# Sliding-window attention feeding a gated FFN: bursts of the fourth unit, weight groups by halves, and the first tile's output groups, on one core

## Chip, core and metric

The kernel runs on one core of a Trainium2 chip. The core has a matrix engine (TensorE, in the profile PE, with its weight loads apart as PEld), a vector engine (VectorE, DVE), an activation engine (ScalarE, ACT), a general engine (GpSimd, POOL) and a queue engine (SyncE, SP) that issues transfers; POOL and ACT issue transfers as well. Each engine works through its own instructions in the order in which the program gives them, and waits on semaphores for the others. The metric is the time of one execution in microseconds of device time. The median of three runs before the change is 301.93 us (301.90 to 302.15).

## What is computed

Causal attention with a window of 64 positions, over 8 batches of 8 heads, 576 positions and head dimension 64; its output, heads side by side, is the input of a feed-forward layer with a ReLU gate (4608 tokens, model width 512, inner width 1536).

```python
scores = (1 / sqrt(64)) * q @ k.T                # per batch and head, 576 x 576
mask = (rel >= 0) & (rel < 64)                   # rel = query position - key position
attn = exp(scores - max) / (sum + 1e-9)          # masked scores are -1e9
x = (attn @ v) as [4608, 512]
out = (maximum(x @ w_gate, 0) * (x @ w_val)) @ w_out
```

Inputs and output are float32. The kernel converts to float16 in the transfers and accumulates in float32.

## The kernel before, in words

**Tiles and units.** The tokens are cut into tiles: four of 384 tokens (tiles 0 to 3), then six of 512. Attention for the first tiles goes by *units* of 192 tokens, three windows of 64 for all 8 heads; units 0 to 2 are batch 0, units 3 to 5 batch 1, units 6 to 8 batch 2. Units 0 and 1 feed tile 0, units 2 and 3 tile 1, and so on. The third unit in the text is unit 2, the fourth unit 3, the fifth to eighth are units 4 to 7. Later attention goes by *quads* of four windows.

**A unit's steps.** `qk_load` (L179, POOL's queue) brings q and k into one of four places of the tile `nats`; `qk_trans` (L199, DVE) transposes them into qT and kT, four transposes a batch: k twice, q twice, a half of the heads each. `u_st` (L265, PE) makes the scores in four banks, `u_exp` (L299, ACT) takes the exponential, `u_mask` (L306, DVE) multiplies by the window's mask, and `u_pv` (L336, PE) multiplies by v into two banks. `u_recip` (L350), `u_norm` (L357) and `u_turn` (L379), all on DVE, normalise and transpose the result into the tile's `xt`. `v_load` (L205, POOL's queue) brings v, and `v_spread` copies some of its rows to the other half of the partitions, on an engine (L215) or by a transfer on SP (L217). `behind_masks` (L312) puts tiny copies on POOL that wait for a unit's masks.

**The FFN of tiles 0 and 1** is the plain product. `hidden` makes gate and value columns in groups: w columns of 128 that fit a bank together (one for 384 tokens, two for 192), four matmuls a column over the 512 of the input (L589). For each block of four columns all gate groups come first (`relu`, L572, ACT), then all value groups (`gate`, L575, DVE). Tile 1 is done in two halves of 192 tokens, because its two units end apart. `output` (L1023) multiplies by w_out: twelve matmuls of 512 columns for 128 tokens, in cuts; then ACT copies the bank (L1035) and SP stores it (L1036). From tile 2 on `fast_hidden` (L634) uses seven products of halves in place of eight. Its operands are sums that `w_form` (L528), `o_form` (L788) and `x_form` (L506) make on DVE and POOL. In the last six tiles the output (`SevenOut`, L847) does the same; there the names P1 to P7 are products, v0 and v1 the attention values of the next tile (`values`, L465), s0 and s1 scores, h1 the start of the next tile.

**Weights.** `w_load` (L159) brings w_gate and w_val in blocks of four columns. Each block is two transfers: a=0 brings the input's chunks 0 and 1, a=1 chunks 2 and 3. `w_done` holds one due time for each column, and `w_need` lets the plan wait for it.

**What sets the order.** A small planner, the `Weaver` W, writes the order out. It has a clock that the code advances by what PE's matmuls are meant to take, and a heap of due actions. `W.at(T, fn)` puts an action in; when the matmul code calls `W.advance`, due actions are issued before the next matmul. So a planned time places an instruction among PE's matmuls, and among the instructions of its own engine; on the chip only queues and semaphores decide. `one_bank` hands out banks 0 to 3 in turn, `two_banks` banks 4 and 5 or 6 and 7; both first issue what still has to read the bank. In the trace the banks 0 to 7 are not told apart.

Of the kernel before, what the change touches and what calls it, by code (L numbers as in the profile page):

```python
# [47 lines left out]
def kernel(  # L48
# [10 lines left out]
    nc = tc.nc  # L59
# [94 lines left out]
    def w_load(wt, src, f0, f1, landed):  # L154

        if wt is not wo:
            ns = slice(128 * f0, 128 * f1)
            for a in range(2):
                nc.gpsimd.dma_start(wt[:, 2 * a:2 * a + 2, ns], src.rearrange("(a p e) n -> a p e n", a=2, e=2)[a, :, :, ns])  # L159
        if wt is wo:  # L160
            nc.gpsimd.dma_start(wo[:, f0:f1], src.rearrange("(c p) n -> p c n", p=128)[:, f0:f1])
        w_done.update(((wt.name, f), landed) for f in range(f0, f1))

    def w_need(wt, f):
        while (wt.name, f) not in w_done:
            W.pop()
        W.advance(w_done[wt.name, f])

# [238 lines left out]
    def part_written(banks):  # L407
        written.update((id(to), 0) for to in banks)
# [145 lines left out]
        while normed[0] < n:  # L554
            W.pop()

    def hidden(t, spans, f0=0, f1=NF, each=1):

        if t not in gs:
            gs[t] = g_sb_p.tile([128, NF, WT], FP16, name="g_sb"), {}  # L560
        g_sb, done = gs[t]
        xt = xt_tile(t)
        n = spans[0][1] - spans[0][0]

        w = 512 // n
        each = max(each, w)

        def part(tile):
            return tile[:, 0:w * n].rearrange("p (w n) -> p w n", w=w)

        def relu(r_sb, h1):
            nc.scalar.activation(part(r_sb), part(h1), ACT.Relu)  # L572

        def gate(f, c0, r_sb, h2):
            nc.vector.tensor_tensor(g_sb[:, f:f + w, c0:c0 + n], part(r_sb), part(h2), MUL)  # L575
            done.update(dict.fromkeys(range(f, f + w), c0 + n))

        for fb in range(f0, f1, each):
            r2s = [f_sb.tile([128, 2, WT], FP32, name="pr", bufs=4) for _ in range(2)]
            r_sbs = {}  # L580
            for i, wt in enumerate((wg, wv)):
                for c0, f in ((c0, f) for c0, _ in spans for f in range(fb, fb + each, w)):
                    h = one_bank()
                    part_written([h])
                    for b in range(w):
                        W.advance(W.clock)
                        w_need(wt, f + b)
                        for c in range(NC):
                            nc.tensor.matmul(h[:, b * n:b * n + n], wt[:, c, (f + b) * 128:(f + b) * 128 + 128],  # L589
                                             xt[:, c, c0:c0 + n], start=(c == 0), stop=(c == NC - 1))  # L590
                        W.clock += 4 * (n + 7) / 2400.0
                    if i == 0:
                        r_sb = r_sbs[c0, f] = r2s[len(r_sbs) // 2][:, len(r_sbs) % 2]
                        W.at(W.clock, lambda r_sb=r_sb, h=h: relu(r_sb, h))
                    else:
                        W.at(W.clock, lambda f=f, c0=c0, r_sb=r_sbs[c0, f], h=h: gate(f, c0, r_sb, h))

    def fast_hidden(t, seven=None):

# [467 lines left out]
    XAT = -0.3  # L1067
    SEVEN_LAST = (("P6", "P5", "P2", "P7", "oP1", "P3", "P4"), ("P6", "P5", "P2", "P7", "oP1", "P4", "P3"))
    SEVEN = {n: ("P2", "v0", "v1", "P6", "P5a", "P7", "s0", "P5b", "P4", "s1", "P3") for n in (-5, -4, -3, -2)}
    SEVEN[-1] = ("v0", "P2", "P6", "v1", "P5a", "P7", "P5b", "P4", "h1", "P3")  # L1070

    SEVEN[0] = ("P2", "P4", "P5", "P6", "P7", "P3")

    with tc.manual_schedule():
# [74 lines left out]
        for u in (4, 5):  # L1149
            v_load(u)  # L1150
        for i, (name, hh) in enumerate((n, hh) for n in "kq" for hh in range(2)):
            W.at(31.6 + 1.4 * i, lambda name=name, hh=hh: qk_trans(1, name, hh))
        for hh, T in enumerate((36.6, 38.8)):
            W.at(T, lambda hh=hh: u_st(3, (hh,)))
            for i in range(G):
                W.at(T + 0.4 + 0.22 * i, lambda hh=hh, i=i: u_exp(3, i, (hh,)))
                W.at(T + 0.8 + 0.22 * i, lambda hh=hh, i=i: u_mask(3, i, (hh,)))
            W.at(T + 3.5 - 0.7 * hh, lambda hh=hh: u_pv(3, (hh,)))
            W.at(T + 4.0 - 0.7 * hh, lambda hh=hh: u_recip(3, (hh,)))
            W.at(T + 4.1 - 0.7 * hh, lambda hh=hh: u_norm(3, hh))  # L1160
            W.at(T + 4.6 - 0.7 * hh, lambda hh=hh: u_turn(3, (hh,)))
        W.at(37.4, lambda: v_spread(3, pool))
        W.at(40.6, lambda: behind_masks(3))

        def pair(t, TA, TB, P):
            for u, T in ((2 * t, TA), (2 * t + 1, TB)):
# [53 lines left out]
        def ahead(t):  # L1220
            T = W.clock
            long = widths[t] == WT
            ends = T + (32.7 if long else 22.5)
            if t + 2 <= LAST:
                qk_turns(t + 2, T, LATE if t - 1 in FAST_OUT else (0.1, 1.4, 8.0, 14.2) if long else (0.1, 1.4, 6.1, 10.7) if t < NS - 1 else (2.4, 6.1, 10.7, 14.2))
                v_ahead(t + 2, ends, ends + VAT if t in FAST_OUT else ends - 5.0 if long else T + 3.0 if t == 2 else ends + 1.5)
# [8 lines left out]
        for T, gap, eng, some in ((40.5, 0.1, nc.gpsimd, sums[0][:4] + sums[1][:3]), (52.8, 0.1, nc.gpsimd, sums[1][3:8]),  # L1235
                                  (48.2, 0.6, nc.vector, sums[0][4:8]), (68.1, 0.1, nc.gpsimd, sums[0][8:]),
                                  (64.5, 0.7, nc.vector, sums[1][8:])):
            for i, (w, j, n) in enumerate(some):
                W.at(T + gap * i, lambda eng=eng, w=w, j=j, n=n: w_form(eng, (wg, wv)[w], n, j))
# [21 lines left out]
        while any(id(one) in unread for one in singles[:4]):  # L1261
# [73 lines left out]
```

## Time and profile before

| | |
|---|---|
| median of three runs | 301.93 us (301.90 to 302.15) |
| the profiled execution's own time | 302.04 us |
| its span, first to last instruction | 300.3 us |
| granted clock of TensorE | 1.000 |
| DMA, mean rate over the span | 111 GB/s |
| tile 2's first matmul of the seven products | 69.08 us |
| head: PE's first wait, for the mask's bias | 4.4 us |

The profile is one execution. Its times count from the first instruction, so the end of the span is 300.3; the rest of the 302.04 lies around it. Each row of a timeline is a run of like instructions: start, length, engine, line, what is written from what, how many, and in brackets the idle time of the engine just before with what ended it. A matmul's record is longer than its turn, because matmuls are pipelined; costs of PE are therefore counted from start to start. A wait is laid to what came last by the records.

DMA is busy from 2 to 59 us almost without a break: POOL's queue brings q, k, v and the weights in a fixed order. The gate weights of the third block are issued at 17.31 and 18.00, the value weights at 19.07 and 20.34.

### The profile page before, as it was taken

To read this page: it belongs to the slowest core of one execution; us is meant where nothing else is said; L and a number is where in the kernel's file an instruction comes from. 1 tells how busy PE (TensorE), PEld (TensorE's weight loads), DVE (VectorE), ACT (ScalarE), POOL (GpSimd) and SP (SyncE) were. 2 spreads that over 40 slices of the span, in tenths; PEclk is the share of its full clock that TensorE was granted. 3 is DMA by queue.
4 is the path that set the end of the run, shared out by engine and by line. 5 is a ranking of instruction groups with operands and counts; after the bars stand their busy time and mean duration, and the time that the engine had idled before them with its cause. 6 is when DMAs were issued, how large, how long until landed. Compare 5 with 4: busy or idle time off the path is not lost.

```text
span 300.3 us, 11073 instructions
## 1 busy us (share of the span) xinstructions
PE 289.6 (96%) x4643; PEld 239.4 (80%) x4643; DVE 251.7 (84%) x517; ACT 196.0 (65%) x408; POOL 201.7 (67%) x241
## 2 busy tenths in 40 slices
PE   4899999999999999999999999999999999999994
PEld 2475877748957975888888888888888888888894
DVE  5947895997995999789999899989858985896584
ACT  3545336258848848885798579857985698538850
POOL 8767689868957893985957595759375617441750
PEclk9999999999999999999999999999999999999999
DMA  7999999979919636911399239922911210031013
GB/s 216 183 196 194 194 197 179 160 131 241 80 40 181 164 70 149 146 42 38 61 219 120 60 53 219 126 57 53 173 37 35 74 41 0 3 103 41 0 38 105
DMA packets 59506, 33.20 MB, mean 111 GB/s; under 512 B 39552, under 2 KB 53824, under 8 KB 59456
## 3 DMA queue, kind: packets, MB, share of 16 engines
q0 software_dynamic: 46688, 18.29, 52.3%
q1 hardware_dynamic: 12192, 13.75, 15.1%
q8 instruction: 36, 0.59, 0.8%
q10 hardware_dynamic: 576, 0.46, 0.5%
q14 instruction: 14, 0.11, 0.1%
HBM read 37.75 MB, written 9.44 MB: 157 GB/s over the span
## 4 chain that ended last, share of the span: by engine, by line
PE 87%; DMA 5%; POOL 4%; DVE 2%; issue 1%; DVEq 0%; POOLq 0%
PE bank L634 46%; PE bank L847 17%; PE bank L589 7%; PE bank L767 5%; PE bank L1023 5%; PE bank L265 3%; DMA wg<-in_moe_w_gate_dram 3%; PE bank L465 2%; DMA v<-in_v_dram 2%; POOL v L205 1%; PE bank L336 1%; POOL wg L159 1%; DVE g_sb L659 1%; DVE g_sb L797 0%; POOL wv L159 0%
## 5 line engine op out<-in xcount | busy, mean ns | idle before, releaser
L659 POOL TENSOR_TENSOR g_sb<-pr 128x512 f16<-128x512 f32 (+1 forms) x36 | 42.7, 1193 | 43.6 <-ACT pr L676 43.6
L670 DVE TENSOR_TENSOR pr<-bank,pr 128x512 f32<-128x512 f32 (+1 forms) x96 | 58.5, 649 | 3.6 <-PE bank L634 1.9
L653 ACT COPY pr<-bank 128x512 f32<-128x512 f32 (+1 forms) x96 | 49.1, 566 | 13.7 <-PE bank L634 13.5
L659 DVE TENSOR_TENSOR g_sb<-r,bank 128x512 f16<-128x512 f32 (+1 forms) x48 | 31.3, 652 | 23.8 <-ACT r L703 22.4
L847 PEld LDWEIGHTS <-g_sb 128*128 128x128 f16 x444 | 41.8, 98 | 5.2 <-issue 0.2
L634 PE MATMUL bank<-xc,vs 128*128 128x256 f16 (+1 forms) x288 | 41.3, 266 | 0.0
L634 PE MATMUL bank<-xc,us 128*128 128x256 f16 (+1 forms) x288 | 41.3, 266 | 0.0
L634 PEld LDWEIGHTS <-vs 128*128 128x128 f16 x384 | 36.5, 98 | 3.5
L634 PEld LDWEIGHTS <-us 128*128 128x128 f16 x384 | 36.5, 98 | 3.3
L205 POOL DMA_DIRECT2D v<-in_v_dram x41 | 34.7, 866 | 2.2 <-DMA nats<-in_q_dram 1.0
L676 ACT ACTIVATE pr<-pr 128x512 f32<-128x512 f32 (+1 forms) x48 | 29.3, 610 | 9.8 <-DVE pr L670 9.8
L703 ACT ACTIVATE r<-bank 128x512 f32<-128x512 f32 (+1 forms) x48 | 27.7, 577 | 4.8 <-PE bank L634 4.0
L634 PEld LDWEIGHTS <-wg 128*128 128x128 f16 x288 | 27.4, 98 | 3.2
L634 PEld LDWEIGHTS <-wv 128*128 128x128 f16 x288 | 27.4, 98 | 2.6
L634 PE MATMUL bank<-xt,wg 128*128 128x256 f16 (+1 forms) x192 | 27.5, 266 | 0.0
L634 PE MATMUL bank<-xt,wv 128*128 128x256 f16 (+1 forms) x192 | 27.5, 266 | 0.0
L797 POOL TENSOR_TENSOR g_sb<-g_sb,xus 128x512 f16<-128x512 f16 x24 | 27.1, 1148 | 0.0
L847 PE MATMUL bank<-wo,g_sb 128*128 128x256 f16 (+1 forms) x222 | 26.6, 270 | 0.0
L430 ACT ACTIVATE pw<-bank 128x512 f16<-128x512 f32 x48 | 25.3, 605 | 1.1 <-PE bank L265 0.7
L847 PE MATMUL bank<-wts,g_sb 128*128 128x256 f16 (+1 forms) x222 | 25.4, 270 | 0.2 <-DVE xw L484 0.2
L643 ACT COPY bank<-bank 128x512 f32<-128x512 f32 (+1 forms) x48 | 24.6, 553 | 0.0
L572 ACT ACTIVATE pr<-bank 128x384 f32<-128x384 f32 x24 | 11.9, 501 | 15.5 <-PE bank L589 12.5
(107 smaller groups left out, 559.8 us busy)
## 6 DMA issues: line engine op xcount, KB each, us to landing
out_dram<-o_sb SPq DMA_DIRECT2D x30, 256.0 KB, 3.1
nats<-in_k_dram POOLq DMA_DIRECT2D x15, 288.0 KB, 6.1
nats<-in_q_dram POOLq DMA_DIRECT2D x15, 288.0 KB, 8.0
v<-in_v_dram POOLq DMA_DIRECT2D x31, 128.0 KB, 8.2
v<-v SPq DMA_DIRECT2D x27, 66.0 KB, 2.7
v<-v SPq DMA_DIRECT2D x13, 132.0 KB, 2.5
wg<-in_moe_w_gate_dram POOLq DMA_DIRECT2D x6, 256.0 KB, 6.4
wv<-in_moe_w_val_dram POOLq DMA_DIRECT2D x6, 256.0 KB, 8.1
```

The costliest lines, as they stand in the source:

```text
L205: nc.gpsimd.dma_start(v16s[b % 2][lo:hi, g, :, 0:64], v[b, :, 64 * g - 64 + lo:64 * g - 64 + hi].rearrange("h p d -> p h d"))
L430: nc.scalar.activation(d["p"][g].rearrange("p n c -> p (n c)"), d["st"][g], ACT.Exp, scale=scale)
L589: nc.tensor.matmul(h[:, b * n:b * n + n], wt[:, c, (f + b) * 128:(f + b) * 128 + 128], xt[:, c, c0:c0 + n], start=(c == 0), stop=(c == NC ...
L634: nc.tensor.matmul(to[:, HT * m:HT * m + HT], w[:, k, 128 * m:128 * m + 128], x[:, k], start=(first and m == 0 and k == 0), stop=(k == 1), ...
L643: nc.scalar.copy(at[j, "B", i][:, 0:TW], at[j, "A", i][:, 0:TW])
L653: nc.scalar.copy(pr[:, i], at[j, "A", i][:, 0:TW])
L659: eng.tensor_tensor(gh[:, f:f + 2, h], pair(r), pair(v), MUL)
L670: nc.vector.tensor_tensor(pr[:, i], to[:, 0:TW], pr[:, i], ADD)
L676: nc.scalar.activation(pr[:, 0], pr[:, 0], ACT.Relu)
L703: nc.scalar.activation(r, to[:, 0:TW], ACT.Relu)
L797: eng.tensor_tensor(to, x, y, op)
L847: nc.tensor.matmul(at[key][:, QN * m * whole:QN * m * whole + n1 - n0], A[:, 128 * m:128 * m + 128], B[:, c, n0:n1], start=(first and m == ...
```

## The change

There is no new kind of work; the matmuls are the same 4640.

1. *Fourth unit in one burst.* Its scores were issued in two halves (by halves of the heads, due 2.2 apart) and its values in two; each is now one burst. Its exponentials and masks are four of 384 columns where they were eight of 192. The transposes of batch 1 have new due times.
2. *Third weight groups by halves, behind the third unit's values.* The third unit is due 1.2 earlier (values 1.5 earlier), which puts its values ahead of the third block of gate weights. `hidden` takes a table `halves`: the first groups of a block (three gate groups, two value groups of block 8) run chunks 0 and 1 for all of them, then chunks 2 and 3 for all of them, in banks of their own; `w_done` and `w_need` know the two halves apart.
3. *Output of tile 0 side by side.* Three groups of 128 tokens run together in the cuts (0, 4, 8, 12), before the second half of tile 1; before, two did, and the third came behind the second half of tile 1. To make room, the first half of tile 1 is given its banks by a list, which uses banks 4 and 5 once.
4. *Shifts that go with it*: fifth and sixth unit's values due at 55.7 for 54.0; one transpose of batch 2 at 52.9 for 53.6; small copies and weight sums by 1.0; a v load in tile 2 at T+6.5 for T+3.0. In the last tile but one's output, P5a stands ahead of v1 where it stood behind.

As the instructions stand on their engines: PE has the third unit's scores four matmuls earlier, its values four matmuls earlier (ahead of all third gate weights), and the fifth and sixth unit's values ahead of twelve matmuls of tile 1 rather than eight. On DVE both q transposes of batch 2 stand between the two norms of the fifth unit; they stood between the two norms of the sixth. SP's third store of tile 0 stands ahead of the four v transfers that it followed. POOL's order differs in one place, the v load of shift 4.

```diff
-        w_done.update(((wt.name, f), landed) for f in range(f0, f1))
+        w_done.update(((wt.name, f, a), landed - 1.3 * (1 - a)) for f in range(f0, f1) for a in range(2))
...
-    def hidden(t, spans, f0=0, f1=NF, each=1):
+    def hidden(t, spans, f0=0, f1=NF, each=1, halves={}, banks=None):
...
-                for c0, f in ((c0, f) for c0, _ in spans for f in range(fb, fb + each, w)):
-                    h = one_bank()
-                    part_written([h])
-                    for b in range(w):
-                        W.advance(W.clock)
-                        w_need(wt, f + b)
-                        for c in range(NC):
-                            nc.tensor.matmul(h[:, b * n:b * n + n], wt[:, c, (f + b) * 128:(f + b) * 128 + 128],
-                                             xt[:, c, c0:c0 + n], start=(c == 0), stop=(c == NC - 1))
-                        W.clock += 4 * (n + 7) / 2400.0
+                items = [(c0, f) for c0, _ in spans for f in range(fb, fb + each, w)]
+                first = halves.get((fb, i), 1)
+                for group in [items[:first]] + [[item] for item in items[first:]]:
+                    hs = [singles[banks.pop(0)] if banks else one_bank() for _ in group]
+                    part_written(hs)
+                    for cs in ((0, 1), (2, 3)) if len(group) > 1 else (range(NC),):
+                        for (c0, f), h in zip(group, hs):
+                            for b in range(w):
+                                W.advance(W.clock)
+                                w_need(wt, f + b, cs[-1] // 2)
+                                for c in cs:
+                                    nc.tensor.matmul(h[:, b * n:b * n + n], wt[:, c, (f + b) * 128:(f + b) * 128 + 128],
+                                                     xt[:, c, c0:c0 + n], start=(c == 0 and not (len(group) > 1 and b)), stop=(c == NC - 1),
+                                                     skip_group_check=len(group) > 1)
+                                W.clock += len(cs) * (n + 7) / 2400.0
...
-    SEVEN[-1] = ("v0", "P2", "P6", "v1", "P5a", "P7", "P5b", "P4", "h1", "P3")
+    SEVEN[-1] = ("v0", "P2", "P6", "P5a", "v1", "P7", "P5b", "P4", "h1", "P3")
...
-        W.at(23.2, lambda: u_st(2))
-        plan_exps(23.2, 2)
-        plan_values(27.4, 2)
+        W.at(22.0, lambda: u_st(2))
+        plan_exps(22.0, 2)
+        plan_values(25.9, 2)
...
-            W.at(31.6 + 1.4 * i, lambda name=name, hh=hh: qk_trans(1, name, hh))
-        for hh, T in enumerate((36.6, 38.8)):
-            W.at(T, lambda hh=hh: u_st(3, (hh,)))
-            for i in range(G):
-                W.at(T + 0.4 + 0.22 * i, lambda hh=hh, i=i: u_exp(3, i, (hh,)))
-                W.at(T + 0.8 + 0.22 * i, lambda hh=hh, i=i: u_mask(3, i, (hh,)))
-            W.at(T + 3.5 - 0.7 * hh, lambda hh=hh: u_pv(3, (hh,)))
...
+            W.at((32.0, 33.4, 34.8, 36.2)[i], lambda name=name, hh=hh: qk_trans(1, name, hh))
+        W.at(37.9, lambda: u_st(3))
+        for i in range(G):
+            W.at(37.9 + 0.5 + 0.4 * i, lambda i=i: u_exp(3, i))
+            W.at(37.9 + 0.9 + 0.4 * i, lambda i=i: u_mask(3, i))
+        W.at(37.9 + 5.0, lambda: u_pv(3))
...
-        plan_batch(2, (36.5, 36.6, 42.5, 42.6), (52.0, 53.6, 56.9, 57.1))
+        plan_batch(2, (36.5, 36.6, 42.5, 42.6), (52.0, 52.9, 56.9, 57.1))
...
-        pair(2, 46.6, 50.0, 54.0)
+        pair(2, 46.6, 50.0, 55.7)
...
-        hidden(0, ((0, U), (U, TT)), 0, 4, 4)
-        hidden(0, ((0, TT),), 4, NF, 4)
-        hidden(1, ((0, U),), each=4)
-        output(0, (0, 1), (0, 8, NF))
+        hidden(0, ((0, U), (U, TT)), 0, 4, 4, halves={(8, 0): 3, (8, 1): 2})
+        hidden(0, ((0, TT),), 4, NF, 4, halves={(8, 0): 3, (8, 1): 2})
+        hidden(1, ((0, U),), each=4, banks=[0, 1, 4, 5, 2, 3, 0, 1, 2, 3, 0, 1])
+        taken["one"] += 2
+        output(0, (0, 1, 2), (0, 4, 8, NF))
         ready(1)
         hidden(1, ((U, TT),), each=4)
-        output(0, (2,))
         output(1)
```

More of the change, by code (lines that the diff above doesn't have):

```diff
@@ L161, in w_load, with w_need @@
             nc.gpsimd.dma_start(wo[:, f0:f1], src.rearrange("(c p) n -> p c n", p=128)[:, f0:f1])
-        w_done.update(((wt.name, f), landed) for f in range(f0, f1))
-    def w_need(wt, f):
-        while (wt.name, f) not in w_done:
+        w_done.update(((wt.name, f, a), landed - 1.3 * (1 - a)) for f in range(f0, f1) for a in range(2))
+    def w_need(wt, f, a=1):
+        while (wt.name, f, a) not in w_done:
             W.pop()
-        W.advance(w_done[wt.name, f])
+        W.advance(w_done[wt.name, f, a])
     nat = {}
@@ new lines, in hidden @@
+                first = halves.get((fb, i), 1)
[12 more added lines that the diff above has]
+                                W.clock += len(cs) * (n + 7) / 2400.0
+                            if cs[-1] < NC - 1:
+                                continue
+                            if i == 0:
+                                r_sb = r_sbs[c0, f] = r2s[len(r_sbs) // 2][:, len(r_sbs) % 2]
+                                W.at(W.clock, lambda r_sb=r_sb, h=h: relu(r_sb, h))
+                            else:
+                                W.at(W.clock, lambda f=f, c0=c0, r_sb=r_sbs[c0, f], h=h: gate(f, c0, r_sb, h))
@@ L1151 @@
         for i, (name, hh) in enumerate((n, hh) for n in "kq" for hh in range(2)):
[L1152 to L1161 removed]
+            W.at((32.0, 33.4, 34.8, 36.2)[i], lambda name=name, hh=hh: qk_trans(1, name, hh))
[4 more added lines that the diff above has]
+        W.at(37.9 + 5.0, lambda: u_pv(3))
+        for hh in range(2):
+            W.at(37.9 + 5.0 + 0.5, lambda hh=hh: u_recip(3, (hh,)))
+            W.at(37.9 + 5.0 + 0.6 + 0.5 * hh, lambda hh=hh: u_norm(3, hh))
+            W.at(37.9 + 5.0 + 1.7 + 0.5 * hh, lambda hh=hh: u_turn(3, (hh,)))
         W.at(37.4, lambda: v_spread(3, pool))
[L1163 removed]
+        W.at(41.6, lambda: behind_masks(3))
         def pair(t, TA, TB, P):
@@ L1225, in ahead @@
                 qk_turns(t + 2, T, LATE if t - 1 in FAST_OUT else (0.1, 1.4, 8.0, 14.2) if long else (0.1, 1.4, 6.1, 10.7) if t < NS - 1 else (2.4, 6.1, 10.7, 14.2))
-                v_ahead(t + 2, ends, ends + VAT if t in FAST_OUT else ends - 5.0 if long else T + 3.0 if t == 2 else ends + 1.5)
+                v_ahead(t + 2, ends, ends + VAT if t in FAST_OUT else ends - 5.0 if long else T + 6.5 if t == 2 else ends + 1.5)
                 if t + 1 == NS:
@@ L1234 @@
         sums = {w: [(w, j, n) for j in range(NF // 4) for n in (0, 1, 3, 2)] for w in (0, 1)}
-        for T, gap, eng, some in ((40.5, 0.1, nc.gpsimd, sums[0][:4] + sums[1][:3]), (52.8, 0.1, nc.gpsimd, sums[1][3:8]),
+        for T, gap, eng, some in ((41.5, 0.1, nc.gpsimd, sums[0][:4] + sums[1][:3]), (52.8, 0.1, nc.gpsimd, sums[1][3:8]),
                                   (48.2, 0.6, nc.vector, sums[0][4:8]), (68.1, 0.1, nc.gpsimd, sums[0][8:]),
```

5 lines of the change are left out of this document (removed).

## The prediction

> **What bounds the kernel now.** I read the page first: the busy line and the chain that ended last.
>
> ```profile
> PE 289.6 (96%) x4643; PEld 239.4 (80%) x4643; DVE 251.7 (84%) x517; ACT 196.0 (65%) x408; POOL 201.7 (67%) x241
> ...
> PE 87%; DMA 5%; POOL 4%; DVE 2%; issue 1%; DVEq 0%; POOLq 0%
> ```
>
> PE (TensorE) is the bound: it is busy for 96% of the span, 87% of the chain is its own, and the granted clock is 1.000 throughout. The change adds and removes no matmul, so it can only win idle time of PE, or gaps that a busy figure hides. So I read next who PE waits for, over the whole span.
>
> ```profile
> PE bank L589 <- DMA wg<-in_moe_w_gate_dram: 0.7, 2, 0.4
> PE bank L589 <- DVE xt L379: 0.7, 1, 0.7
> PE bank L847 <- DVE xw L484: 0.2, 1, 0.2
> ```
>
> After the head there are only four waits, 1.6 us in all. The change reaches two: one of the two waits for gate weights, and the last. The other weight wait (14.5 us) and the wait for xt (16.5) lie ahead of the first instruction that moves. Then I read PE's timeline around the moved work: start, length, and in brackets the idle time before.
>
> ```profile
> 26.24 0.49 PE L589 MATMUL bank<-xt,wg 128*128 128x384 f16 x2
> 27.09 0.50 PE L589 MATMUL bank<-xt,wg 128*128 128x384 f16 x2 [0.36 <-DMA wg<-in_moe_w_gate_dram]
> 27.52 0.56 PE L336 MATMUL bank<-v,p 128*32 128x65 f16 x48
> 28.01 2.12 PE L589 MATMUL bank<-xt,wg 128*128 128x384 f16 x12
> ...
> 36.66 0.36 PE L265 MATMUL bank<-qT,kT 32*128 32x64 f16 x24
> 37.00 1.48 PE L589 MATMUL bank<-xt,wv 128*128 128x192 f16 x16
> 38.32 0.82 PE L589 MATMUL bank<-xt,wg 128*128 128x192 f16 x8
> 39.08 0.36 PE L265 MATMUL bank<-qT,kT 32*128 32x64 f16 x24
> 39.37 0.83 PE L589 MATMUL bank<-xt,wg 128*128 128x192 f16 x8
> 40.04 0.49 PE L589 MATMUL bank<-xt,wv 128*128 128x192 f16 x4
> 40.47 0.36 PE L336 MATMUL bank<-v,p 128*32 128x65 f16 x24
> 40.76 1.16 PE L589 MATMUL bank<-xt,wv 128*128 128x192 f16 x12
> ```
>
> Lengths overlap, so I count from start to start. Sixteen matmuls of 384 columns take 2.61 us (23.63 to 26.24): 0.163 each. Of 192 columns sixteen take 1.32 (33.92 to 35.24): 0.0825. Of 512 columns 25 take 5.49 with the change of shape behind them: 0.216.
>
> **Third weight groups.** The two matmuls at 26.24 end their turn at 26.57; the next two, on the second half of the same weights, start at 27.09. The stall is 0.52 us. After the change the third unit's values stand first. A whole burst of 48 costs 0.58 with its entry (27.43 to 28.01, same row), so values run from 26.33, the weights begin at 26.82, and three groups take their first halves (6 x 0.163) before any second half is wanted, at 27.80, 0.75 after it landed. The value weights then start at 29.43; two groups' first halves last to 30.08, and the second half landed 9.3 us after its issue at 20.34, at 29.6. Both are covered: **-0.52**. The order of instructions shows the cover that this needs: the third unit's scores stand 4 matmuls (0.65) earlier, its exponentials start near 23.1, its four masks end by about 26.0, and POOL's copies of v end at 25.80. If a mask is late, the values are.
>
> **One burst each.** Fourth unit's scores now: 36.56 (end of the sixteen) to 37.00, and 38.98 to 39.37, together 0.83. One burst costs 0.58: 0.25 won. Values: 40.37 to 40.76 and 41.99 to 42.37, 0.77 against 0.58: 0.19. **-0.44**. The exponentials become 4 of 384 columns for 8 of 192 (1.64 against 1.98 us on ACT), the masks 4 for 8; neither ends a PE wait.
>
> **P5a ahead of v1** (tile 10's output). The 0.18 us before 263.59 is P5a waiting for a bank of the first values. With four matmuls moved ahead, the bank named at that place is another, and the second values need the old one only in their last eighth, 0.57 later. v1 starts 0.44 later, but DVE reaches its reciprocals only at 265.80, so nothing behind it moves: **-0.18**.
>
> **Output of tile 0 side by side** moves 12 matmuls of 512 columns ahead of the second half of tile 1; on PE it is zero-sum. It hands SP a third store of 256 KB near 50.5 instead of 63.8. The v load moved to T+6.5 issues behind a POOL product in tile 2; its data is wanted a tile later: nothing.
>
> **What is late next.** Two waits come near, and both end with DVE.
>
> (i) Scores of the fourth unit now need all four transposes of batch 1. DVE's row from the gate at 31.30 to the last transpose's end at 38.56 holds the same ten operations in either order, 7.26 us. PE arrives at 38.1 (26.82 + 5.22 + 5.32 + 0.66 + 0.09). PE releases that gate at about 30.6 after the change, which gives 38.0 and no wait. But before, the gate was released at 30.8 and started at 31.30; if what held it stays put, the wait is 0.54.
>
> (ii) Scores of the seventh unit need the banks of the sixth's values, and DVE's new order puts both q transposes ahead of the norms that free them.
>
> ```profile
> 60.00 2.31 DVE L199 STREAM_TRANSPOSE qT<-nats 128x576 f32<-128x576 f32 x2
> 62.16 0.54 DVE L357 TENSOR_TENSOR xus<-bank,r 128x384 f16<-128x384 f32 x1
> 62.63 0.53 DVE L575 TENSOR_TENSOR g_sb<-pr,bank 128x384 f16<-128x384 f32 x1
> 63.09 1.01 DVE L379 STREAM_TRANSPOSE xt<-xus 128x384 f16<-128x384 f16 x2
> ```
>
> Before, the last norm ended at 62.7 and PE came at 63.03: 0.3 spare. After, from the start of the second q transpose to the end of the last norm there are, by the spacing of these rows, a transpose 1.08, a norm 0.46, two turns 0.95, two reciprocals 0.19, a norm, a gate and a norm 0.46 + 0.46 + 0.55: 4.15. PE arrives at 62.7 (69.08 - 0.96, less 20 matmuls, one burst and one without entry). So the wait is the transpose's start less 58.55. That start is set by the second q load. It was issued on POOL at 50.26 and landed 9.0 later, at 59.25. POOL's own queue gets there sooner: its last-mask copies ended at 42.56 and now should end between 41.5 and 42.5. Low end: a full 1.0 earlier, when DVE's own queue (second transpose at 58.5) decides and the wait is 0. If the issue gains nothing: 0.73. High end: the third store goes ahead of it. Stores that queue behind one another land up to 1.3 apart (67.44 + 7.0 to 69.89 + 5.8): landing 60.5, wait 2.0. I take a landing half-way between the first two, 58.85, since the issue moves by about half its reach: **+0.35**. A wait at (i) comes out of (ii), so the larger of the two counts.
>
> [...]
>
> Two masks that ran while POOL copied v (24.10 to 25.80) took 1.25 us together; the next two took 0.61. So the earlier masks could lose up to 0.6. Two of them now come before the copies start; the last two and the copies one after the other end at 24.10 + 1.70 + 0.62 = 26.42: values 0.2 late, absorbed in (ii). [...]
>
> **Sum.** -0.52 - 0.44 - 0.18 + 0.35 = -0.79 us. The profiled execution took 302.04 (span 300.3); less 0.79 it is 301.25. The median of the runs is 0.11 lower: **301.1**. About 0.2% (0.6 us) is what a measurement of this kernel can tell from no change.
>
> **Rivals.**
> - *No new wait*: the q load gains its full 1.0. 300.8. For: the packet records show POOL's queue nearly empty from 49 to 51 us, so an earlier issue starts at once. Against: the stores run beside it. Chance 0.15.
> - *The wait eats the gain*: landing between 59.3 and 60.0, wait 0.75 to 1.5, time 301.6 to 302.2. For: DVE is 84% busy and in order, one late load holds everything behind it. Chance 0.20.
> - *Slower*: the third store pushes the second q load past 60.3; from 59.7 on the wait exceeds the 1.14 won. At 60.5 it is 2.0, time 302.8. For: the DMA row is at 9 tenths up to 58 us. [...] Chance 0.08.
> - *The weight stall stays in another form*: values wait for the masks for 0.4 or more, and the wait passes on to (i) with it: 301.6. Chance 0.05.
> - My forecast, a wait of 0.1 to 0.75: 300.9 to 301.5. Chance 0.52.
>
> Faster by over 0.2% (below 301.33): three quarters of the forecast and the first rival, 0.54. Slower: the third rival and a little of the second, 0.10. The rest is same, 0.36. Range 300.7 to 302.3: it leaves out the far end of the slower rival and a little below.
>
> **What would show it.** Right: no weight wait near 27, values at 26.3, the last stage's 0.18 gone, one burst of 48 at about 38.1, and tile 2's first matmul at 68.1 to 68.9 instead of 69.08. Step (ii) is read from PE's wait for the norm (L357) before the seventh unit's scores and from the landing of the second q load. I am wrong if PE waits in tile 2 for DVE or ACT, which now follow a PE that is up to 1 us ahead, or if that load lands past 59.7.

## The result and the profile after

The changed kernel takes 301.25 us (median of ten runs, 300.98 to 302.17) against 301.90 for ten runs of before (301.60 to 302.19). The ratio is 0.998, with a 95% interval of 0.9971 to 0.9988: faster by 0.65 us in the medians, 0.6 by the ratio. The number on record was 301.1. The profiled execution took 301.48 (before 302.04) and spans 299.8 us (before 300.3).

The busy line and the chain of the page:

```profile
PE 289.4 (97%) x4643; PEld 239.6 (80%) x4643; DVE 251.8 (84%) x513; ACT 195.6 (65%) x404; POOL 201.9 (67%) x241
...
PE 94%; DVE 2%; DMA 1%; ACT 1%; issue 0%; DVEq 0%
```

PE's own part of the chain rose from 87% to 94%: the transfer of the gate weights, and POOL's issues of loads ahead of it, are out of it. PE's longest wait, apart from the one for the mask's bias in the head:

```profile
PE bank L593 <- DVE xt L379: 1.4, 1, 1.4
```

The wait for gate weights near 27 and the one for xw (L484) near 263 are gone, as forecast. But the wait in the head that the profile lays to xt, ahead of the first moved instruction, is 1.4 us in place of 0.7. Before, the row was:

```profile
16.50 1.48 PE L589 MATMUL bank<-xt,wg 128*128 128x192 f16 x16 [0.66 <-DVE xt L379]
```

After, in the head and where the work moved:

```profile
17.03 1.48 PE L593 MATMUL bank<-xt,wg 128*128 128x192 f16 x16 [1.35 <-DVE xt L379]
...
26.87 0.56 PE L336 MATMUL bank<-v,p 128*32 128x65 f16 x48
27.36 2.77 PE L593 MATMUL bank<-xt,wg 128*128 128x384 f16 x16
29.97 2.76 PE L593 MATMUL bank<-xt,wv 128*128 128x384 f16 x16
32.57 1.48 PE L593 MATMUL bank<-xt,wg 128*128 128x192 f16 x16
...
38.60 0.55 PE L265 MATMUL bank<-qT,kT 32*128 32x64 f16 x48
...
43.55 0.56 PE L336 MATMUL bank<-v,p 128*32 128x65 f16 x48
```

Third weight groups run without a gap (27.36 + 16 x 0.163 = 29.97), and the fourth unit has one burst of each kind. From start to start the two bursts cost 0.58 (37.85 + 8 x 0.0825 = 38.51, to 39.09) and 0.57 (41.08 + 11 x 0.216 = 43.46, to 44.03), 0.45 less than the four of before (0.83 + 0.77). The values stand at 26.87 and the scores at 38.60, both half a microsecond behind the forecast 26.3 and 38.1, because the second gate group in the head began 0.53 later. On DVE, the rows that answer to those of step (ii):

```profile
57.81 2.33 DVE L199 STREAM_TRANSPOSE qT<-nats 128x576 f32<-128x576 f32 x2
59.98 0.54 DVE L357 TENSOR_TENSOR xus<-bank,r 128x384 f16<-128x384 f32 x1
...
62.51 0.55 DVE L357 TENSOR_TENSOR xus<-bank,r 128x384 f16<-128x384 f32 x1
```

The last norm ends at 63.06 and PE comes to the seventh unit's scores at 63.19: no wait. (Counts of matmuls below go by the trace, which has 4643 in either kernel.) Cut at PE landmarks, the two profiled executions differ so:

| stretch of PE | before | after | difference | predicted |
|---|---|---|---|---|
| start of tile 0's second gate group | 16.50 | 17.03 | +0.53 | 0 |
| from there to tile 1's first matmul | 16.07 | 15.54 | -0.53 | -0.52 |
| from there to tile 2's first matmul (69.08, 68.59) | 36.51 | 36.02 | -0.49 | -0.44 + 0.35 |
| from there to the products at 231.57 (231.26) | 162.49 | 162.67 | +0.18 | 0 |
| from there to the last matmul (296.31, 295.76) | 64.74 | 64.50 | -0.24 | -0.18 |

The three gains came as forecast or a little larger, together 1.26. The give-back of step (ii) did not come. In its place 0.71 us went in two places that the prediction does not know. The third row holds all that the change does between tile 1 and tile 2, the output side by side too, and not the bursts alone. The experiments ask what these are, and what each part is worth outside of this one pair of executions. Each was timed beside the kernel before on its own chip; "before" is the median there.

### The profile page after: what moved, and what is told of

Its sections match the earlier page's. It is cut to its first block, busy times and chain, and to the rows that moved or that the text cites. A ratio compares the mean times of both kernels' runs of the same rounds, so it can differ in the third digit from the quotient of the medians.

```text
span 299.8 us, 11069 instructions
## 1 busy us (share of the span) xinstructions
PE 289.4 (97%) x4643; PEld 239.6 (80%) x4643; DVE 251.8 (84%) x513; ACT 195.6 (65%) x404; POOL 201.9 (67%) x241
## 4 chain that ended last, share of the span: by engine, by line
PE 94%; DVE 2%; DMA 1%; ACT 1%; issue 0%; DVEq 0%
PE bank L641 46%; PE bank L854 18%; PE bank L593 10%; PE bank L774 5%; PE bank L1030 5%; PE bank L265 4%; PE bank L465 3%; PE bank L336 1%; DMA vs<-in_k_dram 1%; DVE qT L199 1%; DVE kT L199 1%; ACT xus L369 0%; PE bank L229 0%; DVE xt L379 0%; ACT nats L192 0%
## 5 line engine op out<-in xcount | busy, mean ns | idle before, releaser
L641 PEld LDWEIGHTS <-wg 128*128 128x128 f16 x288 | 27.4, 98 | 3.2
L641 PEld LDWEIGHTS <-wv 128*128 128x128 f16 x288 | 27.4, 98 | 2.6
```

What stands on the lines that cost most here:

```text
L641: nc.tensor.matmul(to[:, HT * m:HT * m + HT], w[:, k, 128 * m:128 * m + 128], x[:, k], start=(first and m == 0 and k == 0), stop=(k == 1), ...
```

## Experiments

**1. The changed kernel again.** Nothing is edited.

> The changed kernel once more, unchanged. Its profile had two gaps of PE that belong to no step of the change: the second gate group of tile 0 began at 17.03 although the transpose it waits for ended at 16.39 (before: 16.50), and the values of the last but two output had a hole of 0.31 us at 231.1 that no semaphore explains (before: 0.11). Theory S (supply of instructions): the 16 KB instruction transfer on queue 8 stands ahead of both places, and PE goes on 1.3 to 1.4 us after its end (15.74 to 17.03, 229.69 to 231.10). Then in this profile the second gate group begins at the later of 16.50 and the transfer's end plus 1.3 to 1.4, and the two gaps are again at the same matmuls (the 224th and the 3807th). Rival V (plain variation of one execution): the start of that group and the end of the transfer have nothing to do with each other, and the gaps lie elsewhere or nowhere. Time by both: 301.0 to 301.5, ratio to before 0.997 to 0.999.

Measured: 301.24 (before 301.72; ratio 0.9991, 0.997 to 1.0013, wide because two of the eleven executions took 304.74 and 305.70, at granted clocks of 0.987 and 0.986). The 16 KB transfer of instructions (queue 8) ended at 15.46 and the second gate group began at 16.77, 1.31 later. The hole at 231 was absent. So the head agrees with theory S, and the hole varies from one execution to the next. From tile 1 to tile 2 this profile takes 36.22 where the first has 36.02: PE waited 0.19 at 42.89 for a gate on DVE (L575). The changed kernel thus differs by 0.2 in this stretch from one execution to another.

**2 and 3. Shifting PE's instructions by 8 and by 88 matmuls.** Only the number differs:

```diff
         st_tiles(0)
+        for i in range(8):
+            to = units[0]["st"][3]
+            nc.tensor.matmul(to[32 * (i % 4):32 * (i % 4) + 32, 0:65], zero[:, 0:32], zero[:, 0:65],
+                             start=True, stop=True, skip_group_check=True)
         bands()
```

> The changed kernel with 8 such matmuls of zeros ahead of PE's first one. Theory S: the place at which PE needs the next 16 KB moves 8 matmuls ahead, into the first gate group of tile 0 (the 8th of its 16 matmuls, near 14.9 us). PE stands there until 1.3 to 1.4 us after the transfer's end, 16.4 to 17.1, has 8 matmuls (0.67) left of that group, and begins the second group at 17.1 to 17.8 in place of 16.5 to 17.03: 0.5 to 0.7 us more than the changed kernel, 301.7 to 302.0. Rival V: 301.0 to 301.5, no pause inside the first group.

> The changed kernel with 88 small matmuls of zeros (32 columns of weights, 65 of data) ahead of PE's first one, in the time in which PE waits for the mask (2.4 to 4.4 us). They compute nothing that is used and only shift PE's later instructions by 176 places in its stream. Theory S: the places at which PE needs the next 16 KB move 88 matmuls earlier in the work, the first from 16.5 to about 11.7 us, and its transfer is asked for while the queues hold little; the second gate group of tile 0 begins at 16.50 as before, and the hole at 231.1 is 0.11 or less. 0.5 to 0.75 us less than the changed kernel: 300.5 to 300.8. Should the transfer be no earlier (14 to 15 us), PE stands from 11.7 to 16 and the time is 304 or more. Rival V: nothing but idle time is touched, 301.0 to 301.5, and the two gaps stay or go without regard to the transfer.

With 8, PE's timeline in the head:

```profile
13.83 0.33 PE L593 MATMUL bank<-xt,wg 128*128 128x192 f16 x2
14.32 0.67 PE L593 MATMUL bank<-xt,wg 128*128 128x192 f16 x6 [0.16 <-DVE r L350]
16.77 2.14 PE L593 MATMUL bank<-xt,wg 128*128 128x192 f16 x24 [1.78 <-issue]
```

PE stops behind the 8th of the group's 16 matmuls, between the group's two banks, waits for nothing that the profile knows ("issue"), and goes on at 16.77, 1.39 after the transfer's end (15.38). The matmul at which it stands is again the 224th of the stream. That is theory S, to the matmul. The second group begins at 17.43. The profiled execution took 301.81; the median is 302.74 (before 301.72; ratio 1.0032, 1.0016 to 1.0049), above the forecast, with a granted clock of 0.992 to 0.994 in seven of twelve executions.

With 88, the transfer came at 7.28 to 8.25, as expected, and the hole at 231 was absent, but the time is 304.58 (1.009, 1.0057 to 1.0123), outside of both forecasts for a transfer this early. Stretches of the head; the columns are busy times of PE, PEld, DVE, ACT and POOL, then PE's clock:

```profile
8.00:10.00 2.00, 1.20 (x50) 0.78 (x50) 2.00 (x3) 0.63 (x3) 1.32 (x2) 1.00 2.13 152
10.00:12.00 2.00, 1.22 (x50) 0.68 (x50) 1.66 (x3) 1.58 (x8) 0.71 (x1) 0.92 1.78 177
12.00:14.00 2.00, 1.94 (x50) 1.37 (x49) 1.81 (x7) 1.57 (x8) 1.27 (x3) 0.50 1.25 203
```

The first scores began at 8.97 instead of 8.39, PE was busy for 1.2 us in each 2 us from 8 to 12, and the granted clock was 0.50 from 11.7 for 6.83 us. So the question what the head costs at full clock is not answered by this kernel. (What took the clock down is open. In a stretch half as long just ahead of it, 8.28 to 11.70, PE was busy for 2.00 of 3.42 us; in experiment 2 a stretch of 3.42, 15.22 to 18.64, had 1.87 and the clock stayed at 1.00. So the busy time of PE by these records does not decide it alone.) The kernel still told one thing more: PE stopped once again, at its 904th matmul, and with the 88 this is the 992nd of the stream.

```profile
57.81 0.92 PE L336 MATMUL bank<-v,p 128*32 128x65 f16 x80
59.84 0.30 PE L336 MATMUL bank<-v,p 128*32 128x65 f16 x16 [1.10 <-issue]
```

The transfer before it ended at 58.49, 1.35 earlier. The places so far, counted in the stream, are 224, 992 = 224 + 6 x 128 and 3807, one short of 224 + 28 x 128. 128 matmuls with their weight loads are 256 instructions; before and after alike, the 36 transfers of 16 KB come to 129 matmuls each (4643 in all), so I take 256 instructions for one transfer.

**4. P5a behind v1 again** in the last output but one.

```diff
-    SEVEN[-1] = ("v0", "P2", "P6", "P5a", "v1", "P7", "P5b", "P4", "h1", "P3")
+    SEVEN[-1] = ("v0", "P2", "P6", "v1", "P5a", "P7", "P5b", "P4", "h1", "P3")
```

> The changed kernel with the old order in the last output but one: v1 ahead of P5a. By the prediction's step P5a then waits again for a bank of the first values: 0.18 us more (0.18 to 0.24), 301.4 to 301.5, with PE's wait for xw (L484) of 0.2 back near 263. Rival: the wait only stands in for something that is late anyway (the stores of the end), and the time stays at 301.25 within 0.1.

Measured: 301.66 beside 301.24 for experiment 1 on the same chip (ratio to before 1.0003, 0.9981 to 1.0024). The wait is back:

```profile
PE bank L854 <- DVE xw L484: 0.2, 1, 0.2
```

From the products behind 231 to the last matmul it takes 0.23 more than in experiment 1. In the fourteen profiles of this study that stretch is 0.23 longer, within 0.02, in every kernel with the old order. This term is shown in the profiles, and a little larger than forecast (0.18); the medians differ by more than it, and their intervals overlap.

**5. The fourth unit in two halves again**, with the old due times of its steps and of batch 1's transposes (the `for hh, T in enumerate((36.6, 38.8))` loop of the kernel before).

> The changed kernel with the fourth unit in two halves again (scores, exponentials, masks, values, and the old due times of batch 1's transposes). By the prediction's step two bursts of each cost 0.25 and 0.19 more than one: from the second gate group of tile 0 to tile 2's first product of the seven 0.44 us more than in the changed kernel (51.6 there, so 52.0), time 301.6 to 301.8. Rival: the transposes or masks that the whole bursts wait for take part of it back, and the halves cost only 0 to 0.2: 301.2 to 301.4.

Measured: 301.83 (before 301.74; ratio 1.0009, 0.9993 to 1.0026), and 36.55 us from tile 1's first matmul to tile 2's, where the changed kernel has 36.02 and, in experiment 1, 36.22. The cost is 0.33 to 0.53 in that stretch, 0.44 was forecast. The rival's 0 to 0.2 is not what the profile shows; the time of the changed kernel was not taken on this chip.

**6. The third weight groups alone**, put into the kernel before: `halves`, the two due times of a column's weights, and the third unit's due times 22.0 and 25.9.

> The kernel before with one part alone: the third weight groups by halves, and the third unit's scores and values due earlier. By the prediction's step the stall of 0.52 ahead of the second halves goes and nothing else moves: from the second gate group to tile 2's first product of the seven 52.06 in place of 52.58, time 0.5 under before. Rival: the third unit's values now wait for its masks, as they did by 0.22 in one profile of the changed kernel, and only 0.3 is left. If both weight halves come late in this execution, neither shows.

Measured: 302.04 (before 301.74; ratio 1.0008, 0.9998 to 1.0017). No gain at all. Its profile has no weight stall in the third block, 15.67 us from the second gate group to tile 1 (16.07 before), and 36.63 in the next stretch (36.51). The forecast of 0.5 fails in the time, though the stall is gone.

**7. The third output group of tile 0 behind the second half of tile 1 again.**

```diff
-            W.at(45.6, lambda u=u: v_spread(u))
+            W.at(44.6, lambda u=u: v_spread(u))
...
-        output(0, (0, 1, 2), (0, 4, 8, NF))
+        output(0, (0, 1), (0, 8, NF))
...
         hidden(1, ((U, TT),), each=4)
+        output(0, (2,))
         output(1)
```

> The changed kernel with the third group of tile 0's output back behind the second half of tile 1, so that its store leaves near 63 and not near 50.9 (the four v transfers are due 1.0 earlier, so that they keep their place ahead of the stores). The prediction had PE's work zero-sum: 301.25 within 0.15. It tells whose doing the earlier landing of the second q load was (57.3 and 58.9 in two profiles of the changed kernel, 59.25 before, 0.1 to 0.3 apart in issue). [...]

Measured: 301.74 (before 301.74; ratio 0.9996, 0.9987 to 1.0005): undone, no gain over before can be told, where 301.25 within 0.15 was expected. The stretch from tile 1 to tile 2 takes 36.56, 0.54 more than in the first profile of the changed kernel and 0.34 more than in experiment 1, so the part is not zero-sum. Two gaps make up most of the 0.54:

```profile
41.02 2.77 PE L1030 MATMUL bank<-wo,g_sb 128*128 128x512 f16 x11
...
53.48 1.48 PE L593 MATMUL bank<-xt,wg 128*128 128x192 f16 x16
55.08 1.55 PE L593 MATMUL bank<-xt,wv 128*128 128x192 f16 x16
```

Eleven output matmuls took 0.23 more than in the changed kernel (2.54), because the fifth of them is the first that needs the second part of w_out, which landed at 42.08 (with three groups side by side twelve stand ahead of it); and the value groups began 0.28 after 54.80, where 53.48 + 16 x 0.0825 would put them, behind a gate on DVE. The second q load landed 6.4 after its issue, at 56.31. In the other kernels with two stores beside it that took 6.4, 6.3, 7.9 and 9.0; in eight with three stores, the load in the same place, 6.7 to 8.3. The ranges overlap: whose doing the landing is stays undecided, and a delay of 0.5 by the third store would be no more than the load's own spread.

**8. The second q load late.** It is issued behind the three v loads that follow it.

```diff
-        plan_batch(2, (36.5, 36.6, 42.5, 42.6), (52.0, 52.9, 56.9, 57.1))
+        plan_batch(2, (36.5, 36.6, 42.5, 43.2), (52.0, 52.9, 56.9, 57.1))
```

> The changed kernel with the second q load of batch 2 issued behind the three v loads that follow it, one change in POOL's queue alone. It prices the prediction's step (ii), which cost nothing in the changed kernel: there the second q transpose began at 58.9, when VectorE came to it, and PE's wait for the sixth unit's norm was 0 with some 0.1 to spare. The last v load of the three landed at 59.8 to 60.9, so the q load should land at 60 to 61 and the transpose begin 1.1 to 2 later. By step (ii) PE then waits 1.0 to 1.9 for the norm ahead of the seventh unit's scores: 302.2 to 303.1. Rival: the norm was not what PE would have waited for, or other work covers it: under 301.6.

Measured: 303.52 (before 301.74; ratio 1.0062, 1.0043 to 1.0082), above the 302.2 to 303.1 expected. The load landed at 61.14. DVE and then PE:

```profile
61.16 1.26 DVE L199 STREAM_TRANSPOSE qT<-nats 128x576 f32<-128x576 f32 x1 [2.17 <-DMA nats<-in_q_dram]
...
64.78 0.55 DVE L357 TENSOR_TENSOR xus<-bank,r 128x384 f16<-128x384 f32 x1
```

```profile
63.12 0.20 PE L265 MATMUL bank<-qT,kT 32*128 32x64 f16 x2
64.46 0.18 PE L265 MATMUL bank<-qT,kT 32*128 32x64 f16 x1 [1.14 <-DVE xus L357]
65.39 0.52 PE L265 MATMUL bank<-qT,kT 32*128 32x64 f16 x45 [0.74 <-DVE xus L357]
```

By the prediction's rule (transpose's start less 58.55, with PE 0.42 later than assumed there) the wait is 61.16 - 58.97 = 2.19. The stretch grew by 2.24 (38.26 against 36.02; 2.04 against experiment 1). Step (ii)'s mechanism and its size are shown; what the prediction had wrong is the landing it assumed.

**9 and 10. The kernel before, two more profiles.** Nothing is edited.

> The kernel before, unchanged, for a second profile of it. Two times decide whether PE stands ahead of the second halves of the third gate weights: the start of the second gate group of tile 0 (16.50 to 17.03 in the profiles so far, set by the instruction transfer) and the landing of the weights (26.35 to 27.93). They are wanted 10.07 us after that start (26.57 in the first profile, where they landed at 27.05: stall 0.5). Theory L (a race that the first profile happened to lose): the stall is landing less start less 10.07, or 0 where that is negative, and in a typical execution (16.8, 26.6 to 27.0) it is 0 to 0.2. Rival F (a fixed stall, as the prediction took it): 0.4 to 0.55 again, whatever the two times. Time 301.4 to 302.1.

> The kernel before once more, for a third profile. Theory L: stall of the third gate weights equal to their landing less the start of the second gate group less 10.07, or 0. Rival F: 0.4 to 0.55. Time 301.4 to 302.1.

Measured: 302.33 and 302.27 in one execution each, both above the 301.4 to 302.1 expected (median of 17 runs of before on that chip: 301.67). In the first, the weights landed at 27.38 and the group had begun at 16.49: 27.38 - 16.49 - 10.07 = 0.82. The timeline:

```profile
26.24 0.49 PE L589 MATMUL bank<-xt,wg 128*128 128x384 f16 x2
27.43 0.50 PE L589 MATMUL bank<-xt,wg 128*128 128x384 f16 x2 [0.70 <-DMA wg<-in_moe_w_gate_dram]
```

From 26.57 to 27.43 is 0.86. In the second, the group began at 16.75, but its third matmul waited for xt until 17.51, so that it counts as 17.34: the weights, landed at 27.23, were wanted at 27.41, and there was no stall. The stall is a race between PE's head and a transfer: 0.52, 0.86 and 0 in three profiles of one program. Theory L holds, the fixed stall falls.

**11. The changed kernel without the halves.** `halves={}` in both calls of tile 0, the third unit's due times back at 23.2 and 27.4.

> The changed kernel without the part on the third weight groups: groups one after the other, third unit's scores and values at their old places. By the prediction's step (a stall of 0.52 comes back) 301.7 to 301.9. By theory L (the stall is 0 to 0.2 in most executions, and the halves cost up to 0.2 where the values wait for the masks) 301.1 to 301.4, no difference from the changed kernel that can be told.

Measured: 303.19 (before 301.67; ratio 1.0047, 1.0034 to 1.0060). Both theories miss. The third weight groups cost about 0.1 in this profile (landing 26.93, wanted at 16.75 + 10.07 = 26.82), but 38.08 us pass between tile 1 and tile 2:

```profile
56.03 0.49 PE L593 MATMUL bank<-xt,wv 128*128 128x192 f16 x4 [0.26 <-DVE g_sb L575]
...
60.93 0.82 PE L593 MATMUL bank<-xt,wv 128*128 128x192 f16 x8 [0.83 <-DVE g_sb L575]
```

The planner's clock passes the due times of batch 2 at other matmuls, and both q transposes now stand on DVE ahead of a gate whose bank PE needs (57.70 to 60.03, the gate at 60.34). The part can't be undone alone, and this kernel prices a bad order on DVE, not the halves.

**12. The third unit's masks earlier.** Scores and exponentials due at 21.4.

```diff
-        W.at(22.0, lambda: u_st(2))
-        plan_exps(22.0, 2)
+        W.at(21.4, lambda: u_st(2))
+        plan_exps(21.4, 2)
```

> The changed kernel with the third unit's scores and exponentials 0.6 us earlier in the plan (four matmuls of 384 ahead), so that its fourth mask stands ahead of the value gates and not behind the first; its values stay where they are. In the profiles of the changed kernel and its variants the values waited 0 to 0.22 for the last mask. If that is what the halves lose, the start of tile 1 comes 15.54 after the second gate group in every profile (so far 15.54 to 15.76), and the time is 301.0 to 301.25. Rival: the masks only collide earlier with POOL's copies of v, and nothing is won: 301.2 to 301.4.

Measured: 301.47, from 300.83 to 303.17 (before 301.67; ratio 0.9995, 0.9979 to 1.0011). Undecided as to the time. The profiled execution took 302.98, and shows one loss that can spread the times:

```profile
58.49 0.65 PE L336 MATMUL bank<-v,p 128*32 128x65 f16 x56 [1.35 <-issue]
```

PE stopped behind 40 of the 96 matmuls of a burst of values, at its 864th matmul, 224 + 5 x 128. The instruction transfer had run from 56.21 to 57.16, 1.33 earlier. In the changed kernel the same transfer ran from 52.48 to 53.62, and PE came to that matmul 3.02 after its end, without a stop. The masks themselves did what was expected in this one profile: 15.54 from the second gate group (counted from its third matmul, which waited for xt) to tile 1.

## Why the number was right, and which steps were not

The forecast 301.1 is 0.15 from the measured 301.25, and part of that is luck. Of the three gains the first profile shows 1.26 for 1.14; of the give-back of 0.35 it shows nothing; and 0.71 that no step has went to other places. In the profiled pair that makes 0.55 for the 0.79 of the sum.

**Third weight groups, -0.52.** Right for the profile it was read from (-0.53), wrong as a forecast for the kernel. The step took the stall of one execution for a property of the program. It is landing less PE's arrival, and three profiles of before give 0.52, 0.86 and 0. From the second gate group to tile 1 the three take 16.01 in the mean, nine profiles of kernels with the halves (all but that of 88 matmuls ahead, where the clock was low) 15.65: 0.36. Experiment 11, without the halves too, has 15.71 there; with it the difference is 0.28. Alone the part gave nothing in the time. What takes some of it back is the step on the masks: the values waited up to 0.22 for the last one in experiment 4, and 0 in the first profile after. The prediction had "0.2 late, absorbed in (ii)"; with no wait at (ii) it is not absorbed.

**One burst each, -0.44.** Right where it can be read directly: 0.45 by starts in the profile after. The stretch from tile 1 to tile 2, which holds other parts too, is 0.29 to 0.49 shorter than before (36.51) in four profiles: the changed kernel twice (36.02, 36.22), with 8 matmuls ahead (36.13) and with P5a behind v1 (36.02).

**P5a ahead of v1, -0.18.** Right, 0.23 to 0.24.

**Output side by side, nothing.** Wrong in experiment 7: undone it costs 0.34 to 0.54 in its stretch, and in the time no gain over before is left to tell. The step counted PE's matmuls as zero-sum and left out that twelve matmuls between a unit's scores and the next hidden groups give DVE and the w_out transfer time. Its worth and that of the bursts do not add: with either of the two undone the stretch is back at 36.55 or 36.56, as before (36.51). Part of it may be a race as well: in experiment 7 w_out was wanted at 41.88 (41.02 + 4 x 0.216) and landed at 42.08; at the 41.71 of the changed kernel's profile it would have cost nothing. With one profile the shares are open.

**(i), 0 or 0.54.** The lower value came: PE reached the fourth unit's scores at 38.60 without a wait, 0.07 behind the end of the last transpose (38.53).

**(ii), +0.35.** The term that did not come. Its rule was right (experiment 8: 2.19 by the rule, 2.24 measured), its landing of 58.85 was not: 57.30. The load was issued at 50.17, 0.09 earlier than before, and landed 7.1 after the issue where it had taken 9.0. Before, one of the sixteen engines finished 2.1 us behind the other fifteen (57.18 and 59.25), after 0.5. In experiment 1 it landed at 58.88 and the wait was still 0, since DVE came to the transpose no sooner. Thus the first rival's case, no new wait, is what happened. Its time, 300.8, is not: in the profiled pair 0.71 us more than before went to the supply of instructions, 0.53 in the head and 0.18 at 231. The instructions ahead of both places are the same number in both kernels, and both losses vary from one execution to the next: the second gate group began at 16.50, 16.49 and 16.75 in three profiles of before, and at 16.50 to 17.03 in the nine other profiles without matmuls ahead. So I take them for chance and not for a cost of the change, which three profiles of before do not prove.

The high end, the third store ahead of the load and a landing at 60.5, did not occur. The store landed behind the load (58.14 and 57.30), and in no profile with the third store beside the load, and the load in its place in the queue, did the load land past 58.9. Whether the store slows the load, and by how much, experiment 7 could not tell.

**What stays open.** The terms as re-measured (-0.28 to -0.36, -0.29 to -0.49, -0.23) make -0.80 to -1.08, less up to 0.3 for a hole at 231 that comes and goes (0.1 in the first profile of before, 0.3 in the first of after, none in the others). The medians differ by 0.65 and, in experiment 1, by 0.48. The three profiled executions of before (302.04, 302.33, 302.27) lie 0.1 to 0.7 over the medians of its runs, those of the changed kernel (301.48, 301.32) 0.1 to 0.2 over theirs. So a run of before without a profile seems to lose less than its profiles show; where, no run here can tell.

## What to carry to other kernels

A stall that a profile shows ahead of a transfer is a difference of two times that both vary (in three profiles of before, the second gate group's start, as counted in experiments 9 and 10, from 16.49 to 17.34, the landing from 27.05 to 27.38). Before pricing its removal, take the landing and the arrival from two or three executions; here 0.52 was one draw from 0 to 0.86. A step that opens with "PE arrives earlier" should then look at the whole list of transfers that land close to their use, the instruction stream's own among them. And a planner's due times tie parts together: one part taken out (experiments 7 and 11) changed DVE's order, so undoing a part is not the same as its worth.

## What the runs showed of the hardware

**PE stood for want of instructions, for 1.78 us in experiment 2.** Queue 8, which the page names `instruction`, brings 36 transfers of 16 KB (0.59 MB), and 37 in the kernel with 88 more matmuls; 4643 matmuls with as many weight loads are 36.3 times 256. In every profile PE started the 224th matmul of its stream, or one 128 k later, no sooner than 1.27 us after the end of the transfer that belongs to it, and where it stopped there, within 1.50. In the head:

| profile | transfer's end | PE starts the 224th | later by |
|---|---|---|---|
| before | 15.04 | 16.50 | 1.46 |
| before, first extra profile | 15.00 | 16.49 | 1.49 |
| before, second extra profile | 15.33 | 16.75 | 1.42 |
| changed kernel | 15.74 | 17.03 | 1.29 |
| the same again | 15.46 | 16.77 | 1.31 |
| 8 matmuls ahead | 15.38 | 16.77 | 1.39 |
| P5a behind v1 | 15.63 | 17.03 | 1.40 |
| fourth unit in two halves | 15.00 | 16.50 | 1.50 |
| halves alone | 15.49 | 16.76 | 1.27 |
| two output groups | 15.39 | 16.77 | 1.38 |
| second q load late | 15.36 | 16.75 | 1.39 |
| without the halves | 15.29 | 16.75 | 1.46 |
| masks earlier | 15.44 | 16.76 | 1.32 |

The 224th is the first matmul of tile 0's second gate group; with 8 matmuls ahead it is the ninth of the first. That matmul does not need the last transpose of xt, which ended at 16.38 before and 16.39 after, but the one ahead of it (15.53 and 15.54). Experiment 12 shows it: two matmuls of the group ran ahead of the last transpose's end, which was 17.30 there, and the third waited for it:

```profile
16.76 0.33 PE L593 MATMUL bank<-xt,wg 128*128 128x192 f16 x2 [0.23 <-issue]
17.36 1.31 PE L593 MATMUL bank<-xt,wg 128*128 128x192 f16 x14 [0.27 <-DVE xt L379]
```

So the transfer held PE in the head of the kernel before as well: the wait for xt that the prediction reads at 16.5, and the 16.50 that the expectation of experiment 1 took for the earliest start, are the transfer's doing. Had the third matmul of the group run 0.06 behind the last transpose, as in experiment 12, that would have been 16.44 before and 16.45 after. It ran at 16.66 and at 17.19, so by this estimate the supply cost 0.22 before and 0.74 after. The starts take three values only, 16.50, 16.76 and 17.03 within 0.01, some 0.26 apart; why, no run tells.

A transfer took 0.88 to 1.95 us. The first began at 14.1 to 14.8 in every kernel but the one with 88 matmuls ahead, when PE had 4 to 17 matmuls left ahead of the place; late in the kernel, transfers began up to 144 matmuls ahead. What made the first so late, no edit shows. The profile lays such a wait to the last semaphore (1.35 to xt, though the transpose named had ended 0.64 earlier) or to "issue". Three of the four places met so far (the 864th, 992nd and 3807th) lie in bursts of values: 96 matmuls of 0.010 us each with their weight loads use 192 of the 256 instructions in a microsecond. The 864th stopped PE in experiments 2 and 11 as well, 1.37 and 1.46 behind the transfer. The stops took 0.1 (at 231 in the first profile of before) to 1.8 us (in experiment 2) a time.
